# Matmuls without use in the prologue, the weights' loads behind x, and the next batch's first load ahead of the loop

## The chip, the cores and the metric

The kernel runs on one core of a Trainium2 chip. The metric is the device time of one execution in microseconds (us), from the first to the last instruction with what lies around them. It was run three times before the change, and once more with a profile.

The engines have short names in all that follows: PE is the matrix engine (PEld its weight loads), DVE the vector engine, ACT the scalar engine, POOL the engine that also issues the loads that change the type of x, and SP the engine that issues transposes by DMA and the stores of the output. A "q" behind a name (SPq, POOLq) means the queue of that engine's DMA instructions.

## The reference

Attention through 32 inducing points, then a gated feed-forward layer. There are 4 batches of 12416 rows with 128 features; everything is float32 for the caller.

```python
def mab(q, kv):
    s = scale * (q @ kv.transpose(0, 2, 1))
    s = s - s.max(-1, keepdims=True)
    a = np.exp(s)
    a /= a.sum(-1, keepdims=True) + 1e-09
    return a @ kv
h = mab(I, x)            # stage 1: 32 points attend to all rows of a batch
attn = mab(x, h)         # stage 2: each row attends to the 32 points
...
gate = 1.0 / (1.0 + np.exp(-(attn @ w_gate)))      # d_ff = 1536
out = (gate * (attn @ w_val)) @ w_out
```

Stage 1 of a batch needs the whole batch before its result `h` exists; only then can stage 2 of that batch start.

## The kernel before, in words

A batch is 97 chunks of 128 rows, kept as `xn[b]` (rows on partitions, 16 bit) and transposed as `xT[b]`. The chunks form six groups of 16 (`groups[0]` to `groups[5]`) and a seventh of one chunk. Both `xn` and `xT` have two buffers, so batches 0 and 1 have one each.

**Order.** The program is scheduled by hand: each engine runs its instructions in the order in which the program emits them and waits only for what they read and write. An instruction that waits holds up all that is behind it on its engine. POOL's queue holds compute, and the loads of x and of the weights; SP's queue holds the DMA transposes and the stores.

**Prologue (batch 0).** The first group and the single chunk are loaded as float32 in two halves through SP's queue, into the still unused `xn[1]` (`first32`); line 172 casts the first half on DVE and the second on ACT into `xn[0]`. The five other groups come through POOL's queue with the cast in the DMA (`x_load`, line 83). PE first computes `indT`, the transposed and scaled inducing points (line 166); its scaling on DVE (line 167) stands ahead of the first cast. Then a loop over p = -2 to 3 runs four steps of different groups in each round, in this order:

- `x_turn` transposes a group on PE (line 632, 16 small matmuls), and DVE and ACT copy half of it each to `xT[0]` (lines 634, 636);
- `s1_score` (line 210) and `s1_max` (line 222), then `s1_exp` on ACT (line 235) for the group transposed a round before;
- `s1_turn_pe` transposes the weights of the group before that (line 248), copied by DVE (line 254);
- `s1_sum` multiplies the weights of the group before that with its rows (line 270).

`arrival` gives the order of the groups: 0, the single chunk, 1, 2, 3, 4, 5. The last group is transposed behind the loop, twelve chunks and then four. After it the parts are joined to `h`; `hw_fill` multiplies `h` with both weight matrices (line 341, it needs `wg16` and `wv16`), and the first 16 chunks of stage 2 are done at once: four of them for the first block (`a2first`), the others through two DMA transposes to `a2r` (line 564). `keep_on` (line 181) puts matmuls whose result nobody reads into some pauses of this part.

**Main loop.** All remaining work is the feed-forward part, in 97 blocks of four chunks. For each pair of hidden tiles PE fills a gate and a value bank (line 825), ACT takes the tanh (line 843), DVE multiplies the two (line 856, one instruction per step), and PE projects (line 941). Two steps are a slot. Everything else is planned into slots by `at(slot, ...)`: stage 2 of the running batch (scores at line 438), and stage 1 and the loads of the next batches. For batch 1, stage 1 takes its transposed x by DMA transposes on SP (`x_transpose_dma`, line 92). In the first batch's slots these stand at 4, 7, 16, 21, 31, 37 and 12 for the seven groups, and `x_load(1, g)` at 2, 4, 5, 17, 24 and 31 for the six loads. The scores of batch 1's first two groups are planned at slots 9 and 13; PE waits there for the transposed x of groups 0 and 1.

Of the kernel before, what the change touches and what calls it, by code (L numbers as in the profile page):

```python
# [9 lines left out]
F32 = mybir.dt.float32  # L10
# [7 lines left out]
P = 128  # L18
# [9 lines left out]
def kernel(  # L28
# [9 lines left out]
    nc = tc.nc  # L38
# [6 lines left out]
    NG = NCH // GC  # L45
# [20 lines left out]
    ps = ctx.enter_context(tc.tile_pool(name="ps", bufs=1, space=bass.MemoryType.PSUM))  # L66
# [6 lines left out]
    xn, xT = {}, {}  # L73

    def x_load(b, s, first=0):
        c0, n = groups[s]
        if s == 0:
            c0, n = 0, n + NLO
        if b not in xn:
            xn[b] = xnp.tile([P, NCH, C], F16, tag="xn", name=f"xn_{b}")  # L80
        cuts = [c0, c0 + first, c0 + n] if first else [c0, c0 + n]
        for c, e in zip(cuts, cuts[1:]):
            nc.gpsimd.dma_start(xn[b][:, c:e, :], xv[b, :, c:e, :])

    def xT_tile(b):
        if b not in xT:
            xT[b] = xTp.tile([P, NCH, P], F16, tag="xT", name=f"xT_{b}")
# [13 lines left out]
    halves = [(0, (GC + NLO) // 2), ((GC + NLO) // 2, GC + NLO)]  # L101
# [5 lines left out]
    nc.scalar.dma_start(ind32[:], inducing)  # L107


    identf = const.tile([P, P], F32, tag="identf")  # L110
    nc.vector.memset(identf[:], 0.0)
    nc.gpsimd.affine_select(
# [10 lines left out]
    wg16 = const.tile([P, NI, 2, P], F16, tag="wg16")  # L123
    wv16 = const.tile([P, NI, 2, P], F16, tag="wv16")
    wo16 = const.tile([P, NJ, C], F16, tag="wo16")
    x_load(0, 3)
    x_load(0, 4)
    x_load(0, 5, GC - BC)

    ident = const.tile([P, P], F16, tag="ident")  # L130
    nc.vector.tensor_copy(out=ident[:], in_=identf[:])
# [18 lines left out]
    NS = len(groups)  # L150
# [9 lines left out]
    for q in range(2):  # L160
        nc.vector.memset(nm1s[q][:], NEG)
        nc.vector.memset(hsts[q][:, at_col[NG], :], 0.0)

    indT = const.tile([P, m], F16, tag="indT")
    indT_ps = ps.tile([P, m], F32, tag="m", name="indT_ps")
    nc.tensor.matmul(indT_ps[:], ind32[:], identf[0:m, 0:m], start=True, stop=True)
    nc.vector.tensor_scalar_mul(out=indT[:], in0=indT_ps[:], scalar1=SCALE)

    for (c, e), copy in zip(halves, (nc.vector.tensor_copy, nc.scalar.copy)):
        copy(
            out=xn[0][:, c:e, :],
            in_=first32[:, c * C : e * C].rearrange("p (j c) -> p j c", c=C),
        )
# [7 lines left out]
    def s1_sum(b, s, a1, tag):  # L183
        hp = ps.tile([P, C + 1], F32, tag=tag, name="hp_ps")
        s1_sum_pe(b, s, a1, hp, 0, 4)
        return s1_sum_keep(b, s, hp)
# [3 lines left out]
    def at(slot, make, late=False, side=False):  # L190
        plan.setdefault((slot, "side" if side else late), []).append(make)
# [70 lines left out]
    def s1_sum_pe(b, s, a1, hp, k0, k1):  # L262
        c0, n = groups[s]
        ng, w, R = s1_dims(s)
        for k in range(k0, min(k1, w)):
            for cols, src in ((slice(0, C), None), (slice(C, C + 1), ones16[:])):
                for g in range(ng):
                    if b == 0 and src is not None:
                        continue
                    nc.tensor.matmul(  # L270
                        hp[32 * g : 32 * g + 32, cols],
                        a1[:, k, 32 * g : 32 * g + 32],
                        xn[b][:, c0 + g * w + k, :] if src is None else src,
                        start=(k == 0 and src is None),
                        stop=(k == w - 1),
                        skip_group_check=True,
                    )
# [238 lines left out]
    def s2_sum_dve(n, e):  # L516
        sm = s2p.tile([P, GC], F32, tag="sm")
        nc.vector.reduce_sum(out=sm[:, 0:n], in_=e[:, 0:n, :], axis=AX.X)
        sme = s2p.tile([P, GC + NLO], F32, tag="sme")
        nc.vector.tensor_scalar_add(out=sme[:, 0:n], in0=sm[:, 0:n], scalar1=1.0e-9)  # L520
        return sme

    def s2_inverse(n, sme):
        rs = s2p.tile([P, GC + NLO], F32, tag="rs")
        nc.vector.reciprocal(out=rs[:, 0:n], in_=sme[:, 0:n])  # L525
        return rs[:, 0:n]
# [114 lines left out]
    for p in range(-2, NS - 3):  # L641
        if p + 2 < NS - 1:
            x_turn(0, *groups[arrival[p + 2]], ("g2", "v2")[p % 2])
        if p + 1 >= 0:
            s = arrival[p + 1]
            a1T[s] = s1_exp(0, s, s1_score(0, s, ("g1", "v1")[(p + 1) % 2]))
        if p >= 0:
            s = arrival[p]
            a1[s] = s1_turn_copy(s, s1_turn_pe(0, s, a1T[s]))
        if p - 1 >= 0:  # L650
            s = arrival[p - 1]
            s1_sum(0, s, a1[s], "acc")
        if p + 1 == EARLY - 1:

            we = const.tile([P, EARLY], F32, tag="we")
            nc.vector.tensor_reduce(
                out=nml[:, 0:1], in_=nm1[:, 0:EARLY], axis=AX.X, op=ALU.min
            )
            nc.scalar.activation(
                out=we[:], in_=nm1[:, 0:EARLY], func=AF.Exp, bias=nml[:, 0:1], scale=-1.0  # L660
            )
            lw = const.tile([P, EARLY], F32, tag="lwe")
            nc.gpsimd.tensor_tensor(out=lw[:], in0=l1[:, 0:EARLY], in1=we[:], op=ALU.mult)
            add_tree(lw, EARLY, l1l[:, 0:1])
            hpart = [const.tile([P, C], F32, name=f"hpart{k}", tag=f"hpart{k}") for k in range(2)]

            def pool_part(p):
                nc.gpsimd.tensor_scalar_mul(
                    out=hpart[p > 0][:], in0=hst[:, p, 0:C], scalar1=we[:, p : p + 1]
                )  # L670
                if p > 0:
                    nc.gpsimd.tensor_tensor(
                        out=hpart[0][:], in0=hpart[0][:], in1=hpart[1][:], op=ALU.add
                    )

            pool_part(0)
        elif p == EARLY - 1:
            pool_part(1)
            nc.gpsimd.dma_start(wg16[:], moe_w_gate.rearrange("c (i t f) -> c i t f", t=2, f=P))
            nc.gpsimd.dma_start(wv16[:], moe_w_val.rearrange("c (i t f) -> c i t f", t=2, f=P))  # L680
        elif p == EARLY:
            pool_part(2)

    sc, sb, sa = arrival[-1], arrival[-2], arrival[-3]
    c0, n = groups[sc]
# [78 lines left out]
    keep_on(2, "g2")  # L764
    for hf in range(2):
        nc.scalar.copy(out=hw[0][:, ts(hf, NI // 2), :], in_=hw_ps[hf][:])
    rs_a = s2_inverse(BC, s2_sum_dve(BC, e_a))
    a2n_a = [
        s2_spread(BC // 2, e_a[:, j : j + BC // 2, :], rs_a[:, j : j + BC // 2], nc.vector)
# [147 lines left out]
    acc = [None]  # L917
    queue = []
    for t in range(NST):
        st = steps[t]  # L920
        i = st["block"]
# [47 lines left out]
    for b in range(B):  # L969
        o = base[b]  # L970
        more = b + 1 < B

        if b == 0:
            plan_stage2(0, groups[1][0], o, None, o + 3, soon=True)
            plan_stage2(0, groups[2][0], o + 5, o + 7, o + 18)
        for s in range(3 if b == 0 else 2, NG - 1):
            k = o + (16 * s - 28 if more else LATE[s - 2])
            plan_stage2(b, groups[s][0], k, k + 2, k + (14 if more else 10))
        k = o + (56 if more else LATE[-2])
        plan_stage2(b, groups[NG - 1][0], k, k + 2, k + 10, far=o + (52 if more else LATE[-1]))  # L980
        if not more:
            continue
        early = (
            [(9, (18, 19, 19)), (13, (27, 27, 27))]
            if b == 0
            else [(8, (15, 16, 17)), (12, (18, 19, 19))]
        )
        later = (
            [(24, (35, 35, 35)), (28, (43, 43, 43)), (40, (48, 49, 49)), (44, (50, 51, 51))]
            if b == 0  # L990
            else [(24, (31, 31, 31)), (28, (35, 35, 35)), (40, (47, 48, 49)), (44, (50, 51, 51))]
        )
        alone = 47 if b == 0 else 43
        for s, (score, total) in enumerate(early + later + [(32, (alone, alone, alone))]):
            plan_stage1(b + 1, s, o + score, [o + e for e in total])
        plan_combine(b + 1, o + 52, o + 55, [(o + 72, o + 74), (o + 80, o + 82)])
        plan_stage2(b + 1, groups[0][0], o + 67, o + 70, o + 78)
        plan_stage2(b + 1, groups[1][0], o + 84, o + 86, o + 94)
        for g in range(NS):
            when = 3 * g if b else (4, 7, 16, 21, 31, 37, 12)[g]  # L1000
            at(o + when, lambda b=b, g=g: x_transpose_dma(b + 1, g))
            if b == 0 and g < NG:
                at(o + (2, 4, 5, 17, 24, 31)[g], lambda g=g: x_load(1, g))
        if b + 2 < B:
            for g in range(NG):
                when = ((24, 33, 42, 60, 60, 82) if b else (33, 37, 60, 60, 78, 82))[g]
                at(o + when, lambda b=b, g=g: x_load(b + 2, g))
# [62 lines left out]
```

## Time and profile before

| | |
|---|---|
| three runs | 725.38, 726.45, 726.51 us (median 726.45) |
| the profiled execution | 725.82 us, span 724.0 us |
| busy in the span | DVE 703.0, ACT 678.5, PE 646.4, POOL 444.0 us |
| chain that ended last | DVE 49%, no visible wait 20%, PE 18%, ACT 9%, DMA 3% |
| mean granted clock of PE | 0.998 |

Times in the profile count from the span's start. A row of the order of time gives the start, the duration, the engine, the line, the operation, the tile written and the tiles read, the shape and the count of merged instructions, and in brackets the idle time of the engine before it and what ended that. A row of a stretch gives its bounds and length, the busy time and count of each engine, then the granted clock (1.00 is full speed), the busy share of the DMA engines and their GB/s. A row of DMA issues gives the tiles, the queue, the size and the time from issue to landing. A row of the chain gives a start, a duration and what the end of the program waited for in it.

### The profile page before, as it was taken

The numbers are of one execution on the slowest core, as the hardware profiler recorded it, in microseconds if no ns is written. First come the engines' busy times: TensorE is split into PE (matmuls) and PEld (weight loads), VectorE is DVE, ScalarE is ACT, GpSimd is POOL, SyncE is SP. The second block draws the span as 40 slices with busy tenths as digits, with TensorE's granted clock in tenths as the row PEclk, the third lists the DMA queues.
The fourth block names the chain that finished last, engine by engine and source line by source line (L and its number), as shares of the span: only waits on it lengthen the run. The fifth ranks groups of instructions, "written<-read, shape, count | busy, mean of one in ns | idle before, by whom it ended". The sixth has DMA issues, their size and how long they took to land.

```text
span 724.0 us, 21498 instructions
## 1 busy us (share of the span) xinstructions
PE 646.4 (89%) x8422; PEld 393.8 (54%) x8422; DVE 703.0 (97%) x868; ACT 678.5 (94%) x1024; POOL 444.0 (61%) x719
## 2 busy tenths in 40 slices
PE   6879898999998988999988989999999999999897
PEld 4445555555555555555555545555555555555555
DVE  4889999999999999999999999999999999999997
ACT  4779999999999999999999999999999999999996
POOL 2562845788754648488657275387866787676220
PEclk9999999999999999999999999999999999999999
DMA  9589597244559372425169440421222122122111
GB/s 208 86 155 159 110 186 111 57 111 92 104 99 165 76 135 71 77 75 119 51 113 164 102 90 31 89 63 43 76 60 70 36 74 62 43 74 67 39 45 46
DMA packets 117894, 65.77 MB, mean 91 GB/s; under 512 B 101376, under 2 KB 102048, under 8 KB 117792
## 3 DMA queue, kind: packets, MB, share of 16 engines
q1 hardware_dynamic: 112176, 50.90, 31.4%
q0 software_dynamic: 5296, 13.34, 11.3%
q8 instruction: 66, 1.08, 0.6%
q14 instruction: 36, 0.29, 0.1%
q10 hardware_dynamic: 320, 0.15, 0.1%
HBM read 27.80 MB, written 25.43 MB: 74 GB/s over the span
## 4 chain that ended last, share of the span: by engine, by line
DVE 49%; issue 20%; PE 18%; ACT 9%; DMA 3%; DVEq 1%; ACTq 0%; POOL 0%; SPq 0%; POOLq 0%
DVE u L856 46%; ACT t L843 8%; PE acc_ps L941 8%; PE v_ps L825 7%; DVE nm L222 2%; DMA xn<-in_x_dram 1%; DMA xT<-xn 1%; PE g_ps L825 1%; PE xt_ps L632 1%; DVEq L856 1%; PE hp_ps L270 1%; ACT a1T L235 1%; DVE xT L634 0%; PE s_ps L438 0%; PE s_ps L210 0%
## 5 line engine op out<-in xcount | busy, mean ns | idle before, releaser
L856 DVE SCALAR_TENSOR_TENSOR u<-t,v_ps 128x1024 f16<-128x1024 f16 (+1 forms) x771 | 671.7, 943 | 3.2 <-PE g_ps L825 1.5
L843 ACT ACTIVATE t<-g_ps 128x1024 f16<-128x1024 f32 (+1 forms) x770 | 590.0, 822 | 26.9 <-ACT t L843 11.8
L825 PE MATMUL v_ps<-a2r,hwt 32*128 32x512 f16 (+1 forms) x1179 | 291.3, 372 | 62.3 <-DVE u L856 60.1
L941 PE MATMUL acc_ps<-wo,u 128*128 128x128 f16 x4620 | 325.6, 220 | 0.1
L941 PEld LDWEIGHTS <-u 128*128 128x128 f16 x4620 | 260.5, 98 | 88.2 <-issue 87.4
L825 PE MATMUL g_ps<-a2r,hwt 32*128 32x512 f16 (+1 forms) x1179 | 294.3, 377 | 0.0
L825 PEld LDWEIGHTS <-hwt 32*128 32x128 f16 x2382 | 91.5, 91 | 194.0 <-issue 148.1
L507 POOL TENSOR_TENSOR sum<-e 128x256 f32<-128x256 f16 (+1 forms) x23 | 15.4, 671 | 136.4 <-ACT e L499 133.6
L553 POOL TENSOR_TENSOR a2n<-e,rs 128x2048 f16<-128x2048 f16 (+2 forms) x24 | 86.3, 3594 | 5.6 <-DVE rs L525 3.8
L531 POOL TENSOR_TENSOR near<-sme,minus 128x16 f32<-128x16 f32 (+1 forms) x22 | 65.3, 2966 | 1.8
L960 ACT ACTIVATE o<-acc_ps 128x512 f32<-128x512 f32 x96 | 58.4, 609 | 0.0
L486 POOL TENSOR_SCALAR rise<-rise 128x256 f32<-128x256 f32 (+6 forms) x110 | 51.2, 466 | 9.7
L487 POOL TENSOR_TENSOR top<-top,rise 128x128 f32<-128x128 f32 (+3 forms) x88 | 28.4, 323 | 7.3
L507 POOL TENSOR_TENSOR sum<-sum 128x128 f32<-128x128 f32 (+3 forms) x92 | 28.4, 309 | 7.2
L485 POOL TENSOR_TENSOR rise<-top 128x128 f32<-128x128 f32 (+3 forms) x88 | 27.3, 310 | 6.9
L485 POOL TENSOR_TENSOR rise<-sc 128x256 f32<-128x256 f32 (+1 forms) x22 | 16.2, 738 | 21.0 <-ACT sc L475 20.7
L910 POOL TENSOR_TENSOR xn_spare<-xn_spare 128x512 f16<-128x512 f32 x9 | 11.5, 1274 | 22.4 <-ACT xn_spare L908 22.3
L490 POOL TENSOR_TENSOR sc<-sc,top 128x512 f32<-128x512 f32 (+1 forms) x22 | 23.9, 1085 | 1.7
L905 POOL TENSOR_SCALAR xn_spare<-xn_spare 128x512 f32<-128x512 f16 x9 | 13.4, 1493 | 11.2 <-ACT xn_spare L904 11.2
L438 PEld LDWEIGHTS <-xT 128*128 128x128 f16 x388 | 13.1, 96 | 11.8 <-issue 11.7
L438 PE MATMUL s_ps<-hT,xT 128*128 128x32 f16 x388 | 18.1, 178 | 0.1
L487 POOL TENSOR_TENSOR top<-sc,rise 128x256 f32<-128x256 f32 (+1 forms) x22 | 16.2, 736 | 1.8
(131 smaller groups left out, 292.1 us busy)
## 6 DMA issues: line engine op xcount, KB each, us to landing
out_dram<-o SPq DMA_DIRECT2D x96, 256.0 KB, 2.2
xn<-in_x_dram POOLq DMA_DIRECT2D x19, 512.0 KB, 7.8
xn<-in_x_dram POOLq DMA_DIRECT2D x3, 544.0 KB, 5.6
xn<-in_x_dram SPq DMA_DIRECT2D x1, 576.0 KB, 4.8
xn<-in_x_dram SPq DMA_DIRECT2D x1, 512.0 KB, 3.9
a2r<-a2n SPq DMA_TRANSPOSE x29, 4.4
xn<-in_x_dram POOLq DMA_DIRECT2D x1, 384.0 KB, 13.9
wg<-in_moe_w_gate_dram POOLq DMA_DIRECT2D x1, 384.0 KB, 4.6
```

Source lines behind the costliest of these rows:

```text
L438: nc.tensor.matmul(s2[:, j, :], xT[b][:, c + j, :], hT16[b][:], start=(j == 0), stop=whole and j == j1 - 1, skip_group_check=True,)
L485: nc.gpsimd.tensor_tensor(out=r, in0=far, in1=near, op=ALU.subtract)
L486: nc.gpsimd.tensor_scalar_max(out=r, in0=r, scalar1=0.0)
L487: nc.gpsimd.tensor_tensor(out=top[:, 0:n, 0:w], in0=near, in1=r, op=ALU.add)
L507: nc.gpsimd.tensor_tensor(out=d[:, 0:n, :], in0=src[:, :, 0:w], in1=src[:, :, w : 2 * w], op=ALU.add)
L531: nc.gpsimd.tensor_tensor(out=near[:, 0:n], in0=sme[:, 0:n], in1=minus1[:, 0:n], op=ALU.pow)
L553: eng.tensor_tensor(out=a2n[:, 0:n, :, :], in0=e.unsqueeze(2).to_broadcast((P, n, 4, m)), in1=rs.unsqueeze(2).unsqueeze(3).to_broadcast((P ...
L825: st[what + "end"] = nc.tensor.matmul(pt[:, k, col : col + nb * P], hw[b][r : r + 32, j // 2, :], a2r[r : r + 32, o : o + nb, :].rearrange ...
L843: st["tanh"] = nc.scalar.activation(out=st["t"][:], in_=st["g"][:], func=AF.Tanh, scale=0.5)
L856: u = nc.vector.scalar_tensor_tensor(out=st["u"][:, :, c:e], in0=st["t"][:, :, c:e], scalar=1.0, in1=st["v"][:, :, c:e], op0=ALU.add, op1= ...
L941: nc.tensor.matmul(acc[0][(i // 2) % len(acc[0])][:, i, :], u[:, ts(i, P)], wo16[:, j, :], start=(i in fresh), stop=not any(e[2] == ib and ...
L960: nc.scalar.mul(out=o32[:], in_=acc[0][0][:], mul=0.5)
```

## The change

- A tile of zeros (the first four chunks of `xT[1]`, which nothing else uses yet) is set by DVE ahead of the memset of `identf`. A new helper `idle_on` runs n matmuls of 128x512 on the zeros, whose result nobody reads: eight before `indT`, two after it, and two at the end of each of the rounds p = 0, 1 and 2.
- The second half of the first group is cast on DVE instead of ACT.
- The loads of `wg16` and `wv16` are issued directly behind those of x, no longer in round p = 2 of the loop.
- `x_load(1, 0)` is issued in the prologue, behind the copies of `hw`, no longer in slot 2; the transpose of that group moves from slot 4 to slot 3.

```diff
@@ before identf
+    xT_tile(0)
+    xT_tile(1)
+    zeros = xT[1][:, 0:4, :]
+    nc.vector.memset(zeros, 0.0)
     identf = const.tile([P, P], F32, tag="identf")
...
     x_load(0, 5, GC - BC)
+    nc.gpsimd.dma_start(wg16[:], moe_w_gate.rearrange("c (i t f) -> c i t f", t=2, f=P))
+    nc.gpsimd.dma_start(wv16[:], moe_w_val.rearrange("c (i t f) -> c i t f", t=2, f=P))
...
+    def idle_on(n, tag):
+        w_ps = ps.tile([P, 4, P], F32, tag=tag, name="w_ps")
+        for _ in range(n):
+            nc.tensor.matmul(w_ps[:], zeros[:, 0, :], zeros, start=True, stop=True)
+
+    idle_on(8, "acc")
     indT = const.tile([P, m], F16, tag="indT")
     indT_ps = ps.tile([P, m], F32, tag="m", name="indT_ps")
     nc.tensor.matmul(indT_ps[:], ind32[:], identf[0:m, 0:m], start=True, stop=True)
     nc.vector.tensor_scalar_mul(out=indT[:], in0=indT_ps[:], scalar1=SCALE)
-    for (c, e), copy in zip(halves, (nc.vector.tensor_copy, nc.scalar.copy)):
-        copy(
+    idle_on(2, "acc")
+    for c, e in halves:
+        nc.vector.tensor_copy(
             out=xn[0][:, c:e, :],
...
             s1_sum(0, s, a1[s], "acc")
+        if 0 <= p < NS - 4:
+            idle_on(2, ("g1", "v1")[p % 2])
         if p + 1 == EARLY - 1:
...
             pool_part(1)
-            nc.gpsimd.dma_start(wg16[:], moe_w_gate.rearrange("c (i t f) -> c i t f", t=2, f=P))
-            nc.gpsimd.dma_start(wv16[:], moe_w_val.rearrange("c (i t f) -> c i t f", t=2, f=P))
...
         nc.scalar.copy(out=hw[0][:, ts(hf, NI // 2), :], in_=hw_ps[hf][:])
+    x_load(1, 0)
     rs_a = s2_inverse(BC, s2_sum_dve(BC, e_a))
...
-            when = 3 * g if b else (4, 7, 16, 21, 31, 37, 12)[g]
+            when = 3 * g if b else (3, 7, 16, 21, 31, 37, 12)[g]
             at(o + when, lambda b=b, g=g: x_transpose_dma(b + 1, g))
-            if b == 0 and g < NG:
-                at(o + (2, 4, 5, 17, 24, 31)[g], lambda g=g: x_load(1, g))
+            if b == 0 and 0 < g < NG:
+                at(o + (None, 4, 5, 17, 24, 31)[g], lambda g=g: x_load(1, g))
```

## The prediction

> **What bounds the kernel now.** I read the page's first and fourth parts, then busy time by stretches, then the order of time where a stretch is not full.
>
> ```profile
> PE 646.4 (89%) x8422; PEld 393.8 (54%) x8422; DVE 703.0 (97%) x868; ACT 678.5 (94%) x1024; POOL 444.0 (61%) x719
> ...
> 0.00:31.00 31.00, 23.25 (x298) 14.72 (x298) 18.76 (x58) 17.29 (x39) 11.83 (x34) 1.00 0.83 160
> 48.00:56.00 8.00, 5.56 (x54) 3.29 (x51) 5.24 (x8) 4.70 (x8) 6.83 (x16) 0.79 1.09 212
> 56.00:100.00 44.00, 39.10 (x560) 23.72 (x558) 43.98 (x54) 42.43 (x65) 20.05 (x34) 1.00 0.82 140
> ```
>
> A stretch's row gives the busy time of PE, weight loads, DVE, ACT and POOL, then granted clock and DMA. From 56 us on DVE is full (43.98 of 44; of its 724.0 - 703.0 = 21.0 us of idleness 12.2 lie before 31 us and 2.8 at 48 to 56), so hardly anything that the change does before 56 us is lost again behind it. The rest is spread thin or lies at the end. Time can be won in two places only: the prologue (0 to 31 us) and the hole of 8.00 - 5.24 = 2.76 us at 48 to 56 us. The change touches both.
>
> The hole, in order of time:
>
> ```profile
> 36.62 5.30 DMA xn<-in_x_dram
> 41.94 9.26 DMA xT<-xn
> 51.24 0.40 PE L210 MATMUL s_ps<-xT,indT 128*32 128x512 f16 x4 [2.44 <-DMA xT<-xn]
> 51.69 0.69 DVE L222 TENSOR_REDUCE nm<-s_ps 128x1 f32<-128x512 f32 x1 [1.61 <-PE s_ps L210]
> 54.00 6.62 DVE L856 SCALAR_TENSOR_TENSOR u<-t,v_ps 128x1024 f16<-128x1024 f16 x7 [1.02 <-PE g_ps L825]
> 53.00:53.50 0.50, 0.50 (x8) 0.26 (x8) 0.00 (x0) 0.00 (x0) 0.41 (x2) 0.50 0.69 99
> ```
>
> The next batch's first x is asked for at 36.62, lands at 41.9, and its transpose takes 9.26 more. PE stands 2.44 us before the first score of that batch (it came there at 48.8), DVE behind it 1.61. The granted clock is then 0.50, which costs DVE a second wait of 1.02.
>
> The prologue:
>
> ```profile
> 0.82 0.17 DVE L111 MEMSET identf<- 128x128 f32 x1 [0.82 <-PEq L1054]
> 1.40 3.47 POOL L83 DMA_DIRECT2D xn<-in_x_dram  x6
> 4.15 0.60 PE L166 MATMUL indT_ps<-identf,ind 32*128 32x32 f32 x2 [4.15 <-DMA ind<-in_inducing_dram]
> 4.89 0.76 DVE L172 CAST xn<-xn 128x1024 f16<-128x1024 f32 x1
> 6.04 1.15 ACT L172 CAST xn<-xn 128x1152 f16<-128x1152 f32 x1 [3.58 <-DMA xn<-in_x_dram]
> 7.25 1.25 PE L632 MATMUL xt_ps<-ident,xn 128*128 128x128 f16 x10 [0.61 <-ACT xn L172]
> 8.43 1.01 ACT L636 COPY xT<-xt_ps 128x1024 f16<-128x1024 f16 x1 [1.23 <-PE xt_ps L632]
> 10.03 1.89 PE L632 MATMUL xt_ps<-ident,xn 128*128 128x128 f16 x16
> 12.47 1.91 PE L632 MATMUL xt_ps<-ident,xn 128*128 128x128 f16 x16
> 15.10 1.07 PE L632 MATMUL xt_ps<-ident,xn 128*128 128x128 f16 x16
> 17.06 1.07 PE L632 MATMUL xt_ps<-ident,xn 128*128 128x128 f16 x16
> 19.18 0.84 PE L632 MATMUL xt_ps<-ident,xn 128*128 128x128 f16 x12
> ```
>
> Sixteen equal transposes take 1.91 us at 12.47 and 1.07 at 15.10. PE ran slow by a factor of 1.79 until about 14.4, after 4.3 us of unbroken work. The clock column shows 1.00 there (first row above), so only the durations tell it. After the first group's two parts (the second at 7.25), the transposes of x begin at 10.03, 12.47, 15.10, 17.06 and 19.18. What they wait for last is PE itself, not x:
>
> ```profile
> xn<-in_x_dram POOLq DMA_DIRECT2D x1, 512.0 KB, 7.0
> xn<-in_x_dram POOLq DMA_DIRECT2D x1, 384.0 KB, 13.9
> ```
>
> The first of the six loads issued from 1.40 on (0.58 each) lands at 8.4. The fifth, issued at 3.7, lands at 17.6. Between them the groups come some 2.3 us apart, in order; the small sixth follows some 0.6 later (an estimate: 128 KB at 2.3 us for 512). So the last big transpose could start at 17.6 at the earliest: the prologue can win 19.18 - 17.6 = 1.6 us and no more.
>
> **The change, part by part.** *Matmuls at the start.* The memset of the zeros stands ahead of that of identf; by the row of 0.17 it takes between 0.17 and four times that (four times the columns). PE starts at 1.1 to 1.6. Pace of such matmuls:
>
> ```profile
> 24.72 1.04 PE L181 MATMUL w_ps<-xT,ident 128*128 128x512 f16 x4
> 26.27 0.59 PE L181 MATMUL w_ps<-xT,ident 128*128 128x512 f16 x2
> ```
>
> (1.04 - 0.59) / 2 = 0.22 each, slow 0.22 x 1.79 = 0.40. Eight take 3.2 us and end at 4.3 to 4.8. The indT matmul (0.60) ends at 4.9 to 5.4 where it ended at 4.75 before; the first cast, behind indT in DVE's queue, starts at 5.0 to 5.5 instead of 4.89. I take 5.3, end 6.06. The second cast, now DVE's, takes 0.76 x 1152/1024 = 0.86 and ends at 7.0; on ACT it ended at 7.19. So the delay of the first cast is hidden by the landing of the second half (6.04), and is paid only past that. ACT is spared 1.15 us in which it had nothing else to do.
>
> *The clock.* PE is then busy from 1.3 to 7 with small holes, longer than the 4.3 us that it needed before. I take it as fast from the second half on: ten transposes 1.25 / 1.79 = 0.70, copies at 7.75 instead of 8.43. From the copies to the next transpose it was 10.03 - 8.43 = 1.60; the last two scores lose about 0.2 of that, which gives 9.15, above the landing at 8.4. [...]
>
> *Two matmuls in each of three rounds.* The wait inside a round at the fast pace:
>
> ```profile
> 18.50 0.23 PEld L248 LDWEIGHTS <-a1T 128*128 128x128 f16 x4 [0.34 <-ACT a1T L235]
> ```
>
> The round from 17.06 to 19.18 takes 2.12 with 0.34 of waiting for the exponent's result in it. Two matmuls add 0.44; they stand where PE would soon wait, so I count 0.2 net, 2.3 a round. That is x's own pace, so x hides them; without that cover they cost 3 x 0.44 = 1.3. The transposes then start at 9.15, 11.45, 13.75, 16.05 and, after a last round of 2.1, 18.15, each later than its x. Gain at the last: 1.0 us; bounds 1.6 (x) and below nothing (rivals).
>
> *Weights behind x.* Two POOL issues of some 0.6 us each move from 20 us to 4.9. POOL has little there:
>
> ```profile
> 16.95 0.20 POOL L663 TENSOR_TENSOR lw<-l,we 128x3 f32<-128x3 f32 x1 [11.85 <-ACT we L659]
> 20.38 0.55 POOL L680 DMA_DIRECT2D wv<-in_moe_w_val_dram  x1
> wv<-in_moe_w_val_dram POOLq DMA_DIRECT2D x1, 384.0 KB, 5.9
> 27.44 0.34 PE L341 MATMUL hw_ps<-wg,hT 128*32 128x384 f16 x2
> ```
>
> They queue behind x, and by the order of landings above take nothing from it. Now wv lands at 26.3 against its use at 27.44; a prologue 1.0 shorter would use it at 26.4, with 0.1 to spare, so the edit earns nothing by itself but keeps the 1.0 safe. Afterwards it lands near 18.2 + 2 x 1.7 = 21.6 (an estimate from 2.3 us for 512 KB). From 19.18 to the first gate everything is DVE, ACT and PE work at the fast pace and moves up by 1.0 whole.
>
> *Next batch's first x.* Its POOL issue moves ahead of the loop:
>
> ```profile
> 28.75 0.21 POOL L455 TENSOR_TENSOR lo<-nmx,hi 128x12 bf16<-128x12 f32 x1
> 31.63 2.31 POOL L553 TENSOR_TENSOR a2n<-e,rs 128x1024 f16<-128x1024 f16 x1 [2.67 <-DVE rs L525]
> 32.22 2.98 SPq L564 DMA_TRANSPOSE a2r<-a2n  x2
> 37.55 0.39 PE L825 MATMUL g_ps<-a2r,hwt 32*128 32x512 f16 x2
> ```
>
> It passes the POOL work of the first slots. With all 1.0 earlier it issues at 28.0, in POOL's 2.67 us of idleness, and lands 5.3 later at 33.3. On SP its transpose, moved from slot 4 to slot 3, stands behind the two of a2r, which leave the queue at 34.2; the matmuls that read the zeros in its target are over by 17 us. Even at the 9.26 us of now it is done at 43.5, and PE comes to the score at 47.8. The hole goes whole: 2.76 us, the clock's part in it too.
>
> What is late next is the second score, four slots on. A slot is 1.73 us:
>
> ```profile
> 41.72 0.36 PE L438 MATMUL s_ps<-hT,xT 128*128 128x32 f16 x8
> 43.45 0.36 PE L438 MATMUL s_ps<-hT,xT 128*128 128x32 f16 x8
> 42.71 1.15 POOL L83 DMA_DIRECT2D xn<-in_x_dram  x2
> xT<-xn SPq DMA_TRANSPOSE x1, 5.2
> ```
>
> So it is due at 47.8 + 6.9 = 54.7. Its x issues at 42.71 - 1.0 = 41.7, lands after 5.3 at 47.0, and its transpose, 5.2 us as now, is done at 52.2: 2.5 us in hand.
>
> **The sum.** 1.0 + 2.76 = 3.76 us. The profiled execution took 725.82 (span 724.0 and 1.8 around it); three runs gave 725.38, 726.45 and 726.51. From 725.82 the sum gives 722.1, from the median 722.7. I take the mean of the four times, 726.04: 722.3.
>
> **The rivals.**
>
> *The hole moves to the second score.* If the second transpose takes 9.3 as the first does now, beside two loads of x, it ends at 56.3, 1.6 after the score is due. DVE waits 1.6 less what is queued ahead, and the gain falls to about 2.2: 723.8. For it: 9.3 was seen. Against: the first one's load and transpose are out of the way, and this one took 5.2.
>
> *The clock does not open sooner,* because zeros or transposes do not count as work. Then the first transposes gain 0.2, three pairs cost up to 0.8 each at the slow pace, and the last transpose starts between 19.2 and 20.9. Only the hole, less 0 to 1.7, is left: 723.3 to 725.0, 724.2 in the middle. [...] The trace speaks against it: the 4.3 us before PE's fast pace hold little but transposes, and the transposes at 15.10 ran fast.
>
> *Slower: the early x holds up the first transposes of a2r.* Both use the same DMA engines:
>
> ```profile
> a2r<-a2n SPq DMA_TRANSPOSE x1, 2.5
> ```
>
> The first a2r transpose, issued at 31.2, lands after 2.5 and is used at 36.5 (37.55 - 1.0): 2.8 us in hand. It decides from there: if it took 9.3 us, as the one at 41.94 did beside x, it would land at 40.5, PE would stand 4.0, and the clock would cost another 1.0. That is 5.0 lost against 3.76 won: 727.3. Against it: x lands by 33.3, so the two meet for 2 us only.
>
> **Chances.** Forecast 0.68, hole moved 0.12, clock not open 0.14, slower by a2r 0.06. A measurement of this kernel tells about 0.2% (1.45 us) from no change. The forecast, the moved hole and most of the clock case lie beyond it: faster 0.88, same 0.06, slower 0.06. Low end: x's bound of 1.6 + 2.76 from 725.4 gives 721.0. High end: it takes in the moved hole and the middle of the clock case and stops at 724.6, short of the rest.
>
> **What the next profile should show.** Right: the transposes of x near 0.70 for ten at 7 us and 1.07 for sixteen from 9.2 on, the last at about 18.2; no wait for xT at the score of 48 us, a granted clock of 1.00 there, DVE full from 31 us. Wrong: sixteen transposes of 1.9 us after 9 us (the clock case), a wait for xT at 54 us (the moved hole), PE waiting for a2r at 37 us (slower).

## The result and the profile after

The changed kernel took 722.25 us in the median of 18 runs (721.99 to 725.13), the kernel before 725.93 in 18 runs beside them; the ratio is 0.996, with a 95% interval of 0.995 to 0.9969. That is 2.9 us less (2.3 to 3.6) by the means; the medians lie 3.7 us apart. The forecast was 722.3. A run more than 1.5% above the fastest of its kernel counts as slow and is left out of the ratios (733.8 us here; 735.8 and 736.6 in the experiments).

The profiled execution of the changed kernel took 725.13 (span 723.4), the longest of its 18, and a second profile of the same kernel 722.2 (span 720.4); the expectations below call them the first and the second look. The two differ in a way that matters, so both are shown. First the busy time by stretches of the first, with columns as before:

```profile
0.00:31.00 31.00, 25.85 (x302) 14.25 (x303) 17.72 (x54) 15.56 (x37) 12.01 (x33) 0.94 0.74 153
48.00:56.00 8.00, 6.85 (x81) 3.96 (x81) 8.00 (x10) 7.88 (x12) 7.40 (x9) 1.00 1.13 202
56.00:100.00 44.00, 39.27 (x565) 23.91 (x564) 43.98 (x54) 42.38 (x64) 22.50 (x41) 1.00 0.77 143
```

The hole at 48 to 56 us is gone whole: DVE is busy for 8.00 of 8.00 us where it had 5.24. The order of time there, and the landing of the transpose:

```profile
31.71 0.58 POOL L83 DMA_DIRECT2D xn<-in_x_dram  x1 [0.30 <-issue]
37.83 3.36 SPq L92 DMA_TRANSPOSE xT<-xn  x1
xT<-xn SPq DMA_TRANSPOSE x1, 5.6
51.19 0.40 PE L223 MATMUL s_ps<-xT,indT 128*32 128x512 f16 x4
58.70 0.40 PE L223 MATMUL s_ps<-xT,indT 128*32 128x512 f16 x4
```

The transposed x lands at 37.8 + 5.6 = 43.4, nearly 8 us before PE comes to the first score, and neither that score nor the second (58.70) has a wait in brackets.

The prologue of the first profile is longer than before, not shorter:

```profile
1.18 3.60 PE L173 MATMUL w_ps<-xT 128*128 128x512 f16 x8 [1.18 <-DVE xT L113]
5.24 0.60 PE L173 MATMUL w_ps<-xT 128*128 128x512 f16 x2
6.20 1.41 PE L645 MATMUL xt_ps<-ident,xn 128*128 128x128 f16 x17 [0.35 <-DVE xn L185]
9.09 1.07 PE L645 MATMUL xt_ps<-ident,xn 128*128 128x128 f16 x16
14.01 1.07 PE L645 MATMUL xt_ps<-ident,xn 128*128 128x128 f16 x16
18.19 1.35 PE L645 MATMUL xt_ps<-ident,xn 128*128 128x128 f16 x16 [1.76 <-DMA xn<-in_x_dram]
21.11 1.36 PE L645 MATMUL xt_ps<-ident,xn 128*128 128x128 f16 x12
xn<-in_x_dram POOLq DMA_DIRECT2D x1, 512.0 KB, 14.7
```

PE is fast from 5.24 on (0.60 for the pair) and transposes sixteen chunks in 1.07 from 9.09 on. But the fourth of POOL's loads, issued at 3.45, needs 14.7 us and lands at 18.15. PE stands for 1.76 us, falls back to the slow pace (1.36 for twelve at 21.11), and the last big transpose starts 1.9 us later than before.

The second profile of the same kernel, and the row of the first gate from the profile before:

```profile
16.44 1.07 PE L645 MATMUL xt_ps<-ident,xn 128*128 128x128 f16 x16
18.72 0.84 PE L645 MATMUL xt_ps<-ident,xn 128*128 128x128 f16 x12 [0.21 <-DMA xn<-in_x_dram]
xn<-in_x_dram POOLq DMA_DIRECT2D x1, 512.0 KB, 13.0
xn<-in_x_dram POOLq DMA_DIRECT2D x1, 384.0 KB, 14.7
30.66 4.52 ACT L857 ACTIVATE t<-g_ps 128x1024 f16<-128x1024 f32 x6 [1.25 <-PE v_ps L839]
```

```profile
31.11 4.52 ACT L843 ACTIVATE t<-g_ps 128x1024 f16<-128x1024 f32 x6 [1.25 <-PE v_ps L825]
```

Here the fourth load lands at 16.4, the fifth at 4.0 + 14.7 = 18.7, and the last big transpose starts behind it at 18.72, held by x for 0.21. Before it was 19.18: 0.46 us won, not 1.0. The tanh of the first gate (line 857, before 843) starts at 30.66, before it was 31.11.

### The profile page after: what moved, and what is told of

It is laid out like the page before. It is cut to its first block, busy times and chain, and to the rows that moved or that the text cites. A ratio compares the mean times of both kernels' runs of the same rounds, so it can differ in the third digit from the quotient of the medians.

```text
span 723.4 us, 21532 instructions
## 1 busy us (share of the span) xinstructions
PE 648.8 (90%) x8438; PEld 392.6 (54%) x8438; DVE 703.6 (97%) x870; ACT 677.6 (94%) x1023; POOL 444.7 (61%) x719
## 4 chain that ended last, share of the span: by engine, by line
DVE 48%; issue 19%; PE 19%; ACT 10%; DMA 2%; DVEq 1%; POOL 0%; ACTq 0%
DVE u L870 45%; ACT t L857 9%; PE acc_ps L955 9%; PE v_ps L839 7%; DMA xn<-in_x_dram 2%; DVE nm L235 2%; PE g_ps L839 1%; DVEq L870 1%; PE hp_ps L283 1%; PE xt_ps L645 0%; PE s_ps L451 0%; POOL xn L83 0%; ACT hwt L433 0%; ACT a1T L248 0%; DVE li L343 0%
## 5 line engine op out<-in xcount | busy, mean ns | idle before, releaser
L451 PE MATMUL s_ps<-hT,xT 128*128 128x32 f16 x388 | 18.1, 178 | 0.1
```

What stands on the lines that cost most here:

```text
L451: nc.tensor.matmul(s2[:, j, :], xT[b][:, c + j, :], hT16[b][:], start=(j == 0), stop=whole and j == j1 - 1, skip_group_check=True,)
```

## The experiments

Each run stands beside runs of the kernel before on its own chip; the median of those is given with it, and the ratio with its 95% interval.

**The changed kernel again.** No edit.

> The changed kernel once more, for a second look at its prologue. Theory A (two gains that add: about 1.0 us in the prologue, where x's landing is then what PE waits for, and 2.76 us from the hole): the late landing of one group of x in the first look (18.15 us) is an accident of that execution; here the groups land some 2.4 us apart, the last big transpose of x starts at 17.9 to 18.5 and the span is near 720.5. Theory B (the weights asked for behind x take their share of x's transfers): the fourth or fifth group is late by 2 us again and the last big transpose starts after 20 us.

722.27 (12 runs) against 725.49; ratio 0.998 (0.9962 to 0.9997; five of the 34 runs before on this chip were themselves at 722.2 to 722.5). The groups land on time in the profiled execution, shown above. Three of the twelve runs lay at 724.9 to 725.0, three of the first eighteen at 723.6 to 725.1. If these are the late landing, as the first profile was, it comes in some executions, and Theory A's "accident of that execution" is too weak a word.

**The early load alone.** The kernel before, with

```diff
         nc.scalar.copy(out=hw[0][:, ts(hf, NI // 2), :], in_=hw_ps[hf][:])
+    x_load(1, 0)
...
-            when = 3 * g if b else (4, 7, 16, 21, 31, 37, 12)[g]
+            when = 3 * g if b else (3, 7, 16, 21, 31, 37, 12)[g]
-            if b == 0 and g < NG:
+            if b == 0 and 0 < g < NG:
...
```

> The kernel before with one part of the change: the next batch's first x asked for ahead of the loop, its transpose in slot 3. Theory A: the hole of 2.76 us at 48 to 56 us goes and the prologue stays as it was: 726.0 - 2.8 = 723.2 us, no wait for xT before 56 us. Rival: nearly the whole gain is from here (722.3), since the prologue is bound by x either way. Second rival: the early load holds up the first transposes of a2r or the hole moves to the second score: 724 or more.

722.46 (11 runs) against 725.49; ratio 0.9964 (0.9953 to 0.9974), 2.6 us less (1.9 to 3.4). No run was above 723.1. So this one edit brings nearly all of the change's gain; on this chip the whole change gave no more (0.998). The time is the first rival's, but Theory A is not refuted by it: its 2.76 us from this chip's 725.49 give 722.7. The profile:

```profile
48.00:56.00 8.00, 6.86 (x86) 3.88 (x82) 8.00 (x11) 7.66 (x13) 6.75 (x17) 1.00 1.13 211
12.44 1.29 PE L632 MATMUL xt_ps<-ident,xn 128*128 128x128 f16 x16
14.45 1.07 PE L632 MATMUL xt_ps<-ident,xn 128*128 128x128 f16 x16
18.53 0.84 PE L632 MATMUL xt_ps<-ident,xn 128*128 128x128 f16 x12
xn<-in_x_dram POOLq DMA_DIRECT2D x1, 384.0 KB, 13.8
30.46 4.52 ACT L844 ACTIVATE t<-g_ps 128x1024 f16<-128x1024 f32 x6 [1.25 <-PE v_ps L826]
```

The hole is gone (8.00). The edit moves a load and a transpose; before, the transpose began at 41.94, as x landed (36.62 + 5.30 = 41.92), so it was the load that held it. And without a single added matmul the prologue ends at 30.46, sooner than in the second profile of the changed kernel: PE's pace changed already inside the transposes at 12.44 (1.29 for sixteen), over a microsecond sooner than in the profile before, and the fifth load landed at 3.8 + 13.8 = 17.6. The last big transpose started at 18.53 with no wait for it, so the rival's reason, a prologue bound by x, is not what the profile shows.

**The matmuls alone.** The kernel before with the zeros, `idle_on(8)`, `idle_on(2)` and the pairs of the rounds; casts and loads as before.

> The kernel before with the matmuls without use alone (eight, two, and two in each of three rounds); the second cast stays on ACT, the weights and the next batch's x stay late. Theory A: the fast pace of PE from about 5 us on, the last big transpose of x at 18.0 to 18.6 instead of 19.2, some 0.7 to 1.0 us less than before: 725.0 to 725.3; the hole stays. Rival: PE fast but nothing won, since x or the casts are late too: 726.0.

726.89 (12 runs, 724.2 to 735.8) against 725.49; ratio 1.0026 (1.0008 to 1.0045): not faster, a little slower. PE was fast and the last big transpose started at 18.57, 0.6 us sooner than before, as Theory A had it. The hole stayed:

```profile
48.00:56.00 8.00, 5.36 (x64) 3.10 (x60) 6.56 (x9) 5.84 (x10) 6.75 (x17) 1.00 1.12 215
50.33 0.40 PE L220 MATMUL s_ps<-xT,indT 128*32 128x512 f16 x4 [2.13 <-DMA xT<-xn]
```

In this execution, a short one (span 722.3), PE waited 2.13 us and its clock stayed at 1.00, so DVE lost 1.44 of 8 us. In the profile before it waited 2.44, the clock went to 0.50, and DVE lost 2.76. The size of the hole differs from execution to execution. No longer run of this kernel was profiled; the one long execution that was, of the kernel without the early load (last experiment), had a far larger hole.

**Without the rounds' matmuls.** The changed kernel, with

```diff
-        if 0 <= p < NS - 4:
-            idle_on(2, ("g1", "v1")[p % 2])
```

> The changed kernel without the two matmuls in each of the three rounds. Theory A as it stood before the result (PE's own work in a round is what spaces the transposes, the two matmuls cost some 0.2 net each): 0.3 to 0.5 us less than the changed kernel. Rival, from its first look (PE waited 0.3 to 0.6 us for x in each round after the two matmuls): they cost nothing, the time is that of the changed kernel within 0.2 us; should PE fall back to the slow pace without them, it is 0.5 us or more slower.

722.56 (12 runs, 722.02 to 725.29) against 725.49; ratio 0.9972 (0.9958 to 0.9986). The lower runs of both kernels are alike (722.0 to 722.4), so the pairs cost nothing, as the rival says; without them PE waits 0.56 and 0.61 us for x in two of the rounds. The profiled execution had the late fourth load again:

```profile
14.08 1.07 PE L645 MATMUL xt_ps<-ident,xn 128*128 128x128 f16 x16 [0.61 <-DMA xn<-in_x_dram]
18.27 1.14 PE L645 MATMUL xt_ps<-ident,xn 128*128 128x128 f16 x16 [2.30 <-DMA xn<-in_x_dram]
```

**Weights late.** The changed kernel with the loads of `wg16` and `wv16` back in round p = 2.

> The changed kernel with the weights' loads where they were before (round p = 2). The first look at the changed kernel and that at the one without the rounds' matmuls both had the fourth of POOL's loads of x landing at 18.1, 1.8 us late, and a time of 725.1; a quarter of all their runs lie there. Theory B (weights behind x let one DMA engine fall behind on x): no run near 725 here, all at 721.9 to 722.5, a mean of 0.7 us less than the changed kernel. Theory A (an accident that has nothing to do with the weights): a quarter of the runs near 725 here as well; and wv may be asked for too late: up to 0.5 us more.

722.33 (6 runs, 722.15 to 722.71) against 726.21; ratio 0.9945 (0.993 to 0.9961). No run near 725, and no loss for asking late, as Theory B has it; six runs, on another chip than the earlier ones, are few for that. The landing of the fifth load is as in the changed kernel's second profile, 14.8 us after its issue at 4.0, and the last big transpose waits for it at 18.78.

**Two loads of x first.** The same, with

```diff
+    x_load(0, 1)
+    x_load(0, 2)
     xT_tile(0)
...
-    x_load(0, 1)
-    x_load(0, 2)
```

> As the kernel with the weights late, and the first two of POOL's loads of x issued ahead of the zeros and identf's mask, at 0.4 instead of 1.6 us. If x's landing is what sets the prologue once PE is fast: the groups land 0.5 to 1.0 us earlier, the last big transpose starts at 17.7 to 18.2 and the time is 721.3 to 721.7. Rival: the first two halves of x share their engines with these loads and land later, the first transposes with them: nothing won or 0.3 us lost (722.2 to 722.5).

722.5 (5 runs, 722.27 to 722.64) against 726.21; ratio 0.9946 (0.9931 to 0.9962). Issued 0.37 us sooner (1.22 instead of 1.59: POOL started late), the loads land no sooner, the fifth at 18.7:

```profile
1.22 1.35 POOL L83 DMA_DIRECT2D xn<-in_x_dram  x2 [0.79 <-POOLq L1068]
18.79 0.84 PE L643 MATMUL xt_ps<-ident,xn 128*128 128x128 f16 x12 [0.19 <-DMA xn<-in_x_dram]
```

The rival's time holds: nothing won. In this profile the landing did not follow the start of the issues.

**The memset alone.** The early load, and the zeros' memset ahead of identf's, no matmuls.

> The kernel with the early load alone, and the memset of the zeros ahead of identf's, without any of the matmuls. With the matmuls x's fifth load landed at 18.6 to 18.7, without them at 17.5. If the memset is the cause (it puts POOL's loads 0.18 us later): 18 or later here. If the matmuls are (they read the zeros and bring the fetch of PE's next instructions forward into x's loads): 17.7 here. The time is that of the early load alone, 722.3 to 722.6, either way.

722.97 (5 runs, 722.5 to 723.2) against 726.21; ratio 0.9952 (0.9936 to 0.9967). The fifth load landed at 4.0 + 14.0 = 18.0, between the two expectations, and the last big transpose started at 19.27, behind PE. So the memset makes at most a part of x's delay; and not even that is shown, since on the same chip the fifth load landed at 3.8 + 14.3 = 18.1 without the memset (next run).

**The early load and the early weights.** No matmuls, old casts; run twice.

> The kernel with the early load alone, and the weights asked for behind x, without matmuls and with the old casts. Theory B: some runs (a tenth to a third) near 725, as in the changed kernel, the others at 722.0 to 722.6. Rival: it takes the matmuls as well, which bring PE's instruction fetch into x's loads at 16.0 to 16.5 us; here it comes later and no run is near 725.

> The early load and the early weights without the matmuls, beside them. If the weights alone bring the late landing: runs 2 to 3 us above the rest here. If it takes the matmuls too (five runs had none): none, all at 722.3 to 723.7.

723.18 (5 runs, 722.92 to 723.7) against 726.21, ratio 0.9956 (0.9941 to 0.9972); and 722.52 (5 runs, 722.23 to 722.9) against 725.95, ratio 0.9954 (0.9942 to 0.9966). In neither profile was one load of x late behind the others; the last big transposes started at 19.22 and 18.80. These two runs lack the memset of the zeros and the cast on DVE as well as the matmuls, so they do not tell which of the three it takes.

**The changed kernel and the one with late weights, side by side.**

> The changed kernel a third time, on the chip of the next three. So far a sixth to a third of its runs lay near 725, the others at 722.0 to 722.6; the same here if the late landing belongs to the kernel and not to a chip.

> The changed kernel with the weights' loads late, beside it. Theory B (weights behind x, with PE's instruction fetch among x's loads, let a group of x land late): no run near 725, 722.1 to 722.7, a mean 0.5 us or more below the changed kernel's if that has its late runs here. Theory A: runs near 725 here too.

The changed kernel 722.67 (5 runs, 722.27 to 723.43), ratio 0.9956 (0.9944 to 0.9968); with late weights 722.33 (5 runs, 722.01 to 723.41), ratio 0.9953 (0.9941 to 0.9964), both against 725.95. The profile of the changed kernel had the late fourth load a third time, that with late weights did not:

```profile
17.95 1.07 PE L645 MATMUL xt_ps<-ident,xn 128*128 128x128 f16 x16 [1.76 <-DMA xn<-in_x_dram]
19.95 0.84 PE L645 MATMUL xt_ps<-ident,xn 128*128 128x128 f16 x12
```

```profile
16.44 1.07 PE L643 MATMUL xt_ps<-ident,xn 128*128 128x128 f16 x16
18.81 0.84 PE L643 MATMUL xt_ps<-ident,xn 128*128 128x128 f16 x12 [0.31 <-DMA xn<-in_x_dram]
19.09 0.55 POOL L693 DMA_DIRECT2D wv<-in_moe_w_val_dram  x1
wv<-in_moe_w_val_dram POOLq DMA_DIRECT2D x1, 384.0 KB, 5.9
27.08 0.34 PE L352 MATMUL hw_ps<-wv,hT 128*32 128x384 f16 x2
```

This time PE kept its pace through the wait (1.07 and 0.84), and the execution took 723.43 instead of 725. Over all runs with the early load: with matmuls and early weights together 11 of 47 lay above 723.4 (8 of them above 724), in every other mixture 2 of 42 (none above 724), with matmuls and late weights 1 of 16. The late load itself was in the profile of three of the four executions of the first sort, and in none of the seven others; the kernel without the early load, below, has matmuls and early weights too, and its profile shows the late load as well. Theory B is what these counts bear out. That it takes the matmuls too rests on ten runs and two profiles, and on a kernel that lacks the memset and the cast besides; and on the two chips that ran late weights no run with the early load lay above 724, the changed kernel's five included, so the chip is not ruled out. With late weights the kernel took 722.33 on both chips, no profile had the late load, and one of eleven runs lay at 723.4; its lead over the changed kernel here (722.67, five runs each) is inside the scatter.

**Without the early load.** The changed kernel with the next batch's first load back in slot 2 and its transpose in slot 4.

> The changed kernel without its early load: matmuls, casts and early weights alone. By the sum on record the hole comes back whole: the changed kernel plus 2.8, 725.0 in undisturbed runs, 1.0 below before. By the run of the matmuls alone (726.9 against 725.5): the hole takes back what the prologue wins, 725.5 to 727, no gain over before; then its trace shows a hole of 2.8 us or more.

726.09 (13 runs) against 725.95; ratio 1.0005 (0.9988 to 1.0023). All the rest of the change together wins nothing while the hole is there. The sum on record asked for 1.0 less than before; the run of the matmuls alone had it right. The runs scatter from 723.9 to 736.6, and the profiled execution is the longest of them, so it does not tell the typical hole. It shows what a large one consists of:

```profile
18.30 1.07 PE L645 MATMUL xt_ps<-ident,xn 128*128 128x128 f16 x16 [1.77 <-DMA xn<-in_x_dram]
xT<-xn SPq DMA_TRANSPOSE x1, 16.5
61.45 0.62 PE L223 MATMUL s_ps<-xT,indT 128*32 128x512 f16 x4 [10.13 <-DMA xT<-xn]
```

The transpose of the next batch's first x, issued at 44.91, took 16.5 us where it took 9.26 before, and PE stood 10.13 us for it. The late fourth load (18.30) was there too. Which of the two takes back what the prologue wins in the other runs is not shown.

## Why the prediction was right, and where it was not

**Right: the hole.** Its place and its cause were as worked out, and its size on average: 8.00 instead of 5.24 us of DVE at 48 to 56 us in the changed kernel and in the early load alone. The early load alone gave 2.6 us (1.9 to 3.4), the sum said 2.76. The hole did not move to the second score. In the eleven profiles with the early load the transpose took 4.8 to 5.6 us and was over before the next two loads of x were issued (at 42.05 to 45.19), so the slack was larger than the bound used. In the three profiles without it the transpose ran beside these loads and took 8.8, 9.26 and 16.5 us, and PE waited 2.13, 2.44 and 10.13 us. So the hole has no fixed size; that the loads beside the transpose make it slow is argued from this, not shown. Six of the 80 runs of the kernel before took 722.2 to 722.5, as if they had no hole, and no trace shows one of them.

**Right: the price to a2r.** The rival that ends slower had the early x delay the first transposes of a2r. In the second profile the first of them took 3.0 us where it took 2.5 before, against 2.8 in hand:

```profile
31.77 2.99 SPq L577 DMA_TRANSPOSE a2r<-a2n  x2
a2r<-a2n SPq DMA_TRANSPOSE x1, 3.0
```

PE did not wait for it.

**Mis-sized: the prologue.** The term was 1.0 us. Where no load of x is late, the first gate starts at 30.50 to 30.75 with the matmuls (five profiles). Without them it starts at 31.11, 30.46, 31.21, 31.16 and 30.74 (before, and the four profiles of the early load without matmuls). The means are 30.67 and 30.94: some 0.3 us. The times scatter around that: 722.27 with them against 722.46 without on one chip, 722.33 against 722.97 and 723.18 on another, 722.67 and 722.33 against 722.52 on the third, so from 0.2 lost to 0.9 won. Two steps of the working failed.

The first is "each later than its x". The landings were taken from the trace before (17.6 for the fifth) and held fixed. With the matmuls the fifth load landed at 18.6 to 18.8 in each of these profiles, without them at 17.6 to 18.1. The last big transpose waited for it in four of the five, so x's bound of 1.6 us had shrunk to 0.5. What delays x is only partly shown. The memset moves POOL's issues by 0.19 us, and with it alone the fifth landed at 18.0, but without it at 18.1 on the same chip. One packet of instructions, taken here for PE's next ones (no profile shows whose they are), moved as well: in the trace before it lies at 17.5 to 18.0, about the landing, in the second profile at 16.0 to 16.5, ahead of it (both answers have the same line):

```profile
q8 instruction: 1, 0.02, 12.2%
```

12.2% of 16 engines over 0.5 us is 0.98 us, if the one packet went through one engine (an estimate). What such a packet costs a load of x no run tests, and that it is this one that delays x is argued from the times, not shown; the first load, which lands long ahead of it, was later too (8.98 to 9.09 in the five with the matmuls, 8.4 to 8.8 without).

The second failing step took PE's slow pace until 14.4 us as the kernel's own. Its end differs from execution to execution. In the four profiles of the early load without matmuls the sixteen transposes from 12.4 to 12.9 us took 1.29 to 1.68 us, not 1.91: the fast pace began inside them. The profile before was the slowest start of the five in this, and the gain was read off against it, so a part of the 1.0 comes in some executions without any matmul added.

**Mis-sized: the weights.** "With 0.1 to spare" moved the use of wv forward by 1.0 but not its issue, which stands in the same loop and moves with it. With the weights late, wv lands at 19.09 + 5.9 = 25.0 and is used at 27.08: 2.1 us in hand. The early issue protected nothing. And "take nothing from it" does not hold in general: the late fourth load was seen only where the weights are early and the matmuls are there. What happens on the DMA engines in it is open; the packet of instructions lies at 16.0 to 16.5 with the late load (first profile) as without it (second).

**The clock.** The rival in which zeros or transposes do not count is refuted: in the first profile, after nothing but zeros and the two small matmuls of `indT`, the pair at 5.24 took 0.60, and the sixteen transposes at 9.09 took 1.07; and the early load alone changed its pace within a stretch that holds little but transposes (12.44). The 4.3 us of unbroken work in the working, read from one profile, are no fixed length. The same eight matmuls start at 1.18 in both profiles, but in the first the two at 5.24 were fast (0.60), in the second those at 5.26 took 1.03 and were still slow. What sets the moment of the change is not shown.

So that 722.3 met the median of 722.25 is partly luck. By the means the gain was 2.9 us (2.3 to 3.6), short of the sum's 3.76. By the medians two errors offset each other: the four experiments with the early load and without the matmuls lie 3.0 to 3.4 us below the kernel before, more than the 2.76 counted for the hole, and the prologue gave about 0.3 where 1.0 was counted, and lost it again in about a quarter of the runs. The kernel before was taken at 726.04 where 18 runs gave 725.93.

## What to carry to other kernels

Look first for a transfer whose late start leaves a hole in the engine that is otherwise full; here moving one load gave nearly all that the whole change gave. When a stage is sped up on one engine, the landings read off the old trace are not a fixed bound: here the fifth came at 18.6 to 18.8 us with the added matmuls and at 17.6 to 18.1 without them, and one load came another 1.8 us later in some executions that also had more queued behind it. And a pace that changes from execution to execution (1.29 to 1.91 us for the same sixteen transposes in five profiles without added matmuls) is to be read from several of them, not from one profile.

## What the runs showed of the hardware

The same wait of PE can be followed by half the clock or by the full one. In the first profile of the changed kernel PE waited 1.76 us for x, and the granted clock was 0.50 from 19.0 to 22.0 us; in the third (side by side with late weights) it waited 1.76 us as well, and the clock stayed at 1.00:

```profile
19.00:19.50 0.50, 0.50 (x10) 0.30 (x7) 0.00 (x0) 0.00 (x0) 0.00 (x0) 0.50 1.09 213
```

```profile
19.00:19.50 0.50, 0.50 (x9) 0.27 (x8) 0.44 (x1) 0.44 (x1) 0.00 (x0) 1.00 1.05 203
```

At the hole a wait of 2.44 us was followed by 0.50 for some 3 us (before), one of 2.13 by 1.00 (the matmuls alone). The clock column shows 1.00 in the first 14 us of the profile before, where sixteen transposes took 1.91 us instead of 1.07: at the start only durations tell the pace. And two loads of x that were issued 0.37 us sooner landed no sooner (one profile).
